# A block with attention and a gated MLP on one core: a one-tile first block, another order of loads and transposes, and more gate tiles inside the attention

## The chip, the core and the metric

The kernel runs on one core of a Trainium2 chip. The core has five engines, each with an instruction queue of its own that it works off in order: TensorE (PE) multiplies matrices out of SBUF into PSUM (eight banks of 128 partitions by 512 floats), VectorE (DVE) and ScalarE (ACT) read and write PSUM and SBUF, GpSimd (POOL) works on SBUF alone, SyncE (SP) issues DMAs. Engines wait for each other by semaphores. The metric is the device time of one execution in microseconds, the median of the runs; lower is better.

## The reference

One sequence of S = 2048 tokens, D = 448 features, all in bfloat16:

```
mod = silu(c) @ w_mod               # six vectors sa, ca, ga, sb, cb, gb of 448
h = layernorm(x) * (1 + ca) + sa
q, k, v = split(h @ wqkv)           # 16 heads of 28
p = softmax(q k^T / sqrt(28)), each query sees itself and the 255 keys before it
x = x + ga * ((p v) @ wo)
h = layernorm(x) * (1 + cb) + sb
z = gelu(h @ w_in)                  # 448 -> 1792
z1, z2 = halves of z;  z2 = layernorm(z2)
g = w_sp @ z2 + b_sp                # over the 2048 tokens
x = x + gb * ((z1 * g) @ w_out)     # 896 -> 448
```

## The kernel before

Tokens lie in 16 tiles of 128. With a window of 256, a query tile j needs the key tiles j-2, j-1 and j. The work goes through these parts, which overlap:

- **Projection by blocks of tiles** (lines 574 to 742): blocks of 2, 2, 2, 2, 4 and 4 tiles. `ln1` takes statistics of each tile on VectorE (line 543), the reciprocal root by a `pow` on POOL (551), and writes the normalised tile `xn`. The tile must then be turned, features on partitions: in the first four blocks by TensorE against an identity, with the eviction applying the modulation (`transp_pe`, 600; evictions at 622 and 626), in the last two by a DMA transpose from SP with a `modulate` on VectorE or POOL behind it (`transp_dma`, 637; 633). `project` (697) makes Q and K in eight chains of four matmuls per block, moving 128 columns per tile of the block, evicted at 718 and 721, and V in four matmuls of 448 columns per tile, evicted at 729 and 732. The weights `WQK` are copied from the loaded `wqk_raw` into padded form first (650 to 659).
- **Attention by query tile** (771 to 843). For each key tile one score block of 16 small matmuls fills two pairs of banks (`s_fn`, 781), one pair for eight heads; one exp on ScalarE evicts a pair (796), so a tile has up to three score blocks and six exps, 90 exps in all. POOL masks the tiles at the edges of the window (804). Eight matmuls multiply an exp's result by V (a PV unit, 809); VectorE divides by the sum (826, 829), a DMA transpose turns the result (833), four matmuls multiply it by `wo` (839), and VectorE adds x (842). Score blocks take their banks from the pairs (0,1), (2,3), (4,5); most projections take single banks from 6, 7, 4, 5.
- **The gated part** (869 to 943). After the second layernorm, z2 of a tile is a `Pair` (662) of chains that share a pass of half-height matmuls, seven passes of 448 columns; z1 of four tiles is seven chains of 512 columns. Their gelu is on ScalarE (899, 918). The tiles in `zraw` (here 0 and 1) are evicted without gelu into the z2 buffer by VectorE or ScalarE (888 to 892), so that the exp table stays loaded, and ScalarE applies gelu there later (895).
- **Mixing over tokens and the output** (970 to 1008). 28 chains of 16 matmuls of 512 columns (980), then the output matmuls (1000), the last addition (1005) and the stores.

The order of all this is not found at run time. Every piece of work is an operation with a number, and the list `ORDER` names them one by one: an engine executes its own operations in the order of the list, `.1` picks another engine where an operation allows one, and the numbers behind a slash pick PSUM banks or buffers. `schedule` (79) reads it, `emit` (102) derives the waits from the data and the buffers. Names such as `qk3_1` (block 3, chain 1), `S2_2` (tile 2, second score block) or `E0_1` (an exp) are those that the code gives to the operations. `warm` operations (1023 to 1027) are matmuls on zeros that fill TensorE's time while the loads come in. Loads (469 to 479) go out from SP, two from ScalarE.

Of the kernel before, what the change touches and what calls it, by code (L numbers as in the profile page):

```python
# [4 lines left out]
ACT = mybir.ActivationFunctionType  # L5
# [50 lines left out]
class Planner:  # L56
# [108 lines left out]
0 16 7 1 21 20 17 18 26 23 28 27 118 120 2 3 1673/0 1674 1675 1676 1677 1678 1679 1680 1681 1682 1683 1684 1685 29/2 1686 1687 1688 1689 1690 1691  # L165
1692 1693 1694 25 30 1695 32/1 33 34 31 8 9 14 6 10 5 4 12 15 13 11 50 119 51 121 54 52 122 53 19 22 55 123 24 56 58/0 124 57 125.2/4 126.2/1 35 1696
1697 1698 1699 1700 36 37 1701 60/0 38 1702 1703 39 59/3 127/0 131/2 40 41 49 46 45 48 47.1 128 61 62.1 63.1 65/1 1704 64 1705 1706 132 1707 1708 1709
66 67 134 129.1 130.1 42 43 44 323 319 321 325 324 326 320 322 327 93/3 88/7 98/0 89 90 103/2 104 99 100 101 91 94 83/1 105 68/6 69 106 70 84 102 92
107 133 85 71 78/7 86 79 95 96 80 81 87.1 72 97 73/0 74 82 75 76 113/6 114 115 116 252 185 77 487/0,1 488/3 491/6 328 329 330.1/1 117.1 333.1/4
332.1/3 489 492 331.1/2 1710 108/4 109 110 1711 140/1 111 141 142 1712 1713 143 145/0 146 147 1714 1715 1716 148 502/1,0 112 155/2 156 157 158 186 254  # L170
253 255 187 402 188 189 404 159.1 403 256 144 149 485/1 135/0 136 1717 137 138 1718 165/2 166 167 168 506/0 503/1 486 509/0,1 139 169 493/0 490 170/2
171 1719 1720 172 180/1 181 182 183 173 160/3 161 162 163 510/7 512/9 184 522/0,1 150/1 151 152 153 494 495/1 257 258 507 504 190 408 406 174.1 191
334 336 337 496/1 335 154.1 505/0 513 511 508 407 514 515/2 405 164 526/10 523/3 529/1,2 530/7 192.1/3 193.1/0 259.1/4 175/1 176 177 178 179.1 516/0
533/1 194/0 195 409 196 197 536/0,1 198/1 199 200.1 201.1 222/3 497/2 498 499 500 207/0 223 208 209 210 224 202/1 203 225 539/4 537/5 211 226 549/0,1
553/8 550/6 260.1/1 531 410 501 932 265/2 204 205 206.1 212/3 232/0 213 214 215 233 266 234 235 216.1 517/1 518 519 520 227/3 521 534 524 411 412 554
527 413.1/3 415.1/0 236 268 267 556/1,0 560/0 557/9 228 229 230 538/0 237/2 217/1 525 238 239 231.1 934 218 219 262/3 261 220 240 532 535 340 241.1
221 264.1 263.1 563/1,0 540 528 564/2 566/4 269/1 242/3 314/2 243 270 315 316 317 244 245 576/1,0 541 933 935 542/2 318.1 936 246.1 577/5 580/3 294/0
295 271 272 296 247/2 297 279/3 248 249 280 281 250 273.1 274/1 275 276 282 277 419 543/1 903 900 902 901 298.1 283.1 278.1 251 583/1,0 284/0 299/2
300 301 302 285 286 287 584/7 587/10 303.1 289/1 290 291 292 288.1 590/1,2 591/1 416.1/2 561 558 414.1/1 551 418 339.1 937 341.1 567/0 555 552 938
293.1 939/2 581 578 941/0 588 585 338.1 559 565 562 593/6 603/1,0 544/1 545 546 547 607/8 604/4 568 569/2 548 917/0 918 919 920 921 922 610/2,0 611/9  # L180
923 924 614/2 925 926 309/1 310 311 312 313.1 579/0 589 617/1,2 594 304/1 305 306 586 307 592 582 947 308.1 420 417 612 423.1 605 615 940 570/1 595
596/1 948 906 618/10 620/0 630/1,0 634/5 631/3 347/1 348 349 352/3 571/2 353 354 355 342/0 350 572 637/0,1 573 574 356.1 421 575 351 638/1 641/6 343
344 345 357/1 358 346.1 644/0,2 359 360 621/0 613 616 606 619 645/7 647/2 657/1,0 661/9 658/4 949 950 361.1 951 362/1 635 608 609 622 623/2 632 942
944.1 952 642 953 956.1/2 954.1/1 422.1 639 662 363 387/2 364 388 389 392/3 393 365 372/0 394 366 664/1,0 668/0 665/10 373 390 391.1 669 367/1 368 369
374 370 371.1 395 396.1 424 375 1410 904 1409 597/3 907 598/2 599 1408 624/2 909 943.1 659 957 955 960.1 666 671/0,1 376 674/8 600 601 636/0 377/1 378
379 648 602 672/5 684/1,2 380 685/2 633 640 646 643 688/7 381.1 691/1,0 625/1 626 627 628 649 650/2 629 397/0 398 399 400 401.1 692/1 695/6 698/2,1
382/1 383 384 385 699/3 908 910 905 651/0 911 912 673/0 701/5 660 675 711/0,2 715/4 712/8 386.1 962 964 663 670 667 963 676 677/1 430/1 431 432 433
718/1,2 652/0 653 654 655 434.1 965 966 656 977 978 450/1 451 719/9 722/10 686 693 945.1 689 696 961.1 713 723 716 958.1 720 725/1,0 678/3 914 913
1415 1414 452 714/0 728/0 435/3 436 437 438 729 460/2 453 461 726/8 454 738/1,0 742/0 727 721 739/8 717 724 425/1 426 427 428 462 463 429 745/1,0 967
439.1 968 971/1 969/0 740 730 731/2 749/9 746/10 694/0 690 679/1 680 681 682 464.1 683 979 980 981 982 743 747 750 702 752/2,0 755/4 697 455/1 456 457  # L190
458 687 753/5 765/1,0 700 459.1 703 704/0 445/1 446 447 448 769/1 766/7 772/2,0 773/3 776/6 946.1 732/1 733/0 734 735 736 970 972 1412 1411 705/0 1413
449.1 737 959 983 994 440/1 441 442 779/2,1 782/2 756/0 744 748 741 443 751 780/4 444.1 792/0,1 754 757 758/1 465/1 466 467 468 796/10 799/1,2 793/8
469.1 995 470/0 471 472 473 800/0 986/0 767 777 984/1 770 774 474.1 803/9 480/1 481 482 483 806/0,1 775/0 778 781 771 783 768 484.1 784 785/2 807/5
809/4 819/2,0 823/3 475/1 476 477 478 804 801 794 797 973.1 479.1 987 976 974 808/0 802 798 820/6 826/0,1 810 795 805 830/1 824 821 831 827/2 759/1
915 985 916 828 760/1 761 762 763 811 812/1 833/1,2 764 1007 1008 836/9 825/0 832 927/1 834/5 846/0,2 847/4 850/0 822 837 835 829 853/1,0 929 838
839/0 857/3 854/8 786/3 813/2 1419 1416 840/1 1417 706/3 707 814/2 708 815 816 709 990.1 991.1 988.1 817 860/0,1 975.1 848 858 851 989.1 855 931 930
928 710 818 992 993 996 863/1 861/10 852/0 787/1 788 789 790 849 873/2,1 859 864 856 862 791 997 998 865 866/2 874/2 877/9 875 880/0,2 841/1 842 843
844 884/7 878 876/0 881/4 1001/0 845 885 999/2 882 879 887/1,2 890/3 888/9 1298/3 1300 1307/4 1301/5 1308 1299 1068/2 1072/3 1309 1310 886 1069 883
1071 1154/1 1070 889 891 1303 1302 1073 1156 1311 1074 1160 1304 1157 1009 1010 1011 1022 1024 1025 1023 1012 1013 1014.1/1 1026 892 893/1 867/2 1002
1000 1076.1 1306 1075.1 1305 1158 1280/4 868/3 1159 1155 869 870 871 1161/1 1077/2 1052/2 1098/3 1284/5 1102 1281 1103 1100 1015 894/0 1016.1/0 1027  # L200
1028 872 1017 1162 1005.1 1003.1 1029/2 1004.1 1427 1436 1030 1163 1164 1079 1031.1/1 1078 1032 1080 1037 1081 1020.1 1056/3 1101 1084/1 1086 1057
1283 1099 1087 1088 1104 1090 1286 1058 1105/0 1282 1285 1055 1089 895/1 1085 1312/2 896 1053 897 1288 1287 1091/3 898 1054 1289/4 1315/5 1292/6 1165
1038 1106 1107 1108 1006.1 1082 1166 1019 1083 1059.1 1060.1 1061/2 899 1039 1290 1294 1317 1314 1321/1 1316 1293 1330/0 1334/7 1331 1318 1327/3 1295
1336 1313 1333 1291 1322 1335 1323 1325 1332 1320 1296 1297 1319 1112/0 1326 1324 1117 1115 1113 1018.1 1021.1 1339/6 1114 1371/2 1329 1328 1337 1040
1041 1092 1093 1042 1043 1109 1094 1095 1062 1063 1432 1437 1035.1 1046/0 1110 1044/1 1033.1 1111 1064 1167 1036 1065 1066 1067 1353/3 1372 1340 1373
1374 1126/2 1341 1354 1130 1342 1116 1338 1375 1118 1132 1359/2 1344/7 1356 1357 1131 1119/1 1343 1127 1196/0 1358 1198 1128 1355 1348/6 1129 1200
1201 1199 1349 1346 1345 1347 1202 1350 1197 1361 1133/0 1360 1420 1439 1426 1047 1045 1433 1425 1121 1049 1120 1122 1134 1048.1 1051.1 1034.1 1096
1050.1 1135 1136 1123 1097 1137 1124 1138 1224/2 1229 1225 1228 1140/3 1141 1143 1227 1226 1203/2 1205 1125 1230 1146 1142 1376/4 1380/5 1378 1144
1351 1231/3 1352 1379 1252/2 1257 1256 1204 1206 1207 1233 1208 1209 1139 1362/7 1145 1147/1 1253 1365/6 1255 1254 1368 1258 1382 1259/0 1366 1364
1367 1381 1394/3 1398/2 1168/2 1363 1377 1395 1399 1170 1370 1383 1384 1369 1396 1172 1169 1403/6 1173 1404 1397 1171 1182/0 1400 1402 1401 1423 1422  # L210
# [873 lines left out]
```

## Time and profile before

| what | value |
|---|---|
| median of 3 runs | 280.18 us (279.99 to 280.56) |
| span of the profiled execution, first to last instruction | 279.1 us |
| PE, ACT, DVE, POOL busy | 268.0, 135.4, 156.1, 94.2 us |
| first exp starts | 17.77 us |
| exps busy | 84.4 us, 90 of them |
| granted TensorE clock | 1.00 in every stage |

The page gives no total of its own for the profiled execution; its span is what the stages are cut from, and the time around the span is taken from the runs' median. Busy shares are averages over stages with different limits, so the table alone does not say what holds the kernel: the chain of waits and the stages do. A row of a timeline reads: start and length in us, engine, line, operation, output <- inputs by the program's names, shape, count. Many rows show line 435, the helper that records every matmul; they are told apart by the tiles' names.

### The profile page before, as it was taken

The numbers are of one execution on the slowest core, as the hardware profiler recorded it, in microseconds if no ns is written. First come the engines' busy times: TensorE is split into PE (matmuls) and PEld (weight loads), VectorE is DVE, ScalarE is ACT, GpSimd is POOL, SyncE is SP. The second block draws the span as 40 slices with busy tenths as digits, with TensorE's granted clock in tenths as the row PEclk, the third lists the DMA queues.
The fourth block names the chain that finished last, engine by engine and source line by source line (L and its number), as shares of the span: only waits on it lengthen the run. The fifth ranks groups of instructions, "written<-read, shape, count | busy, mean of one in ns | idle before, by whom it ended". The sixth has DMA issues, their size and how long they took to land.

```text
span 279.1 us, 6498 instructions
## 1 busy us (share of the span) xinstructions
PE 268.0 (96%) x2750; PEld 142.8 (51%) x2776; DVE 156.1 (56%) x373; ACT 135.4 (49%) x183; POOL 94.2 (34%) x156
## 2 busy tenths in 40 slices
PE   8899999999999988999999999999999999999995
PEld 4667677655565645444344444444444444444452
DVE  5688775576757688597385841332424230433543
ACT  4689999999999999866566600000000000000000
POOL 4166796755568677646322120000000000000000
PEclk9999999999999999999999999999999999999999
DMA  7954129796587683469999700000000000000223
GB/s 240 366 125 76 23 42 203 131 168 161 145 152 133 126 154 77 94 113 169 172 167 189 133 4 0 0 2 0 0 0 0 19 0 0 2 0 0 66 79 105
DMA packets 67503, 25.38 MB, mean 91 GB/s; under 512 B 56337, under 2 KB 67346, under 8 KB 67474
## 3 DMA queue, kind: packets, MB, share of 16 engines
q1 hardware_dynamic: 67200, 24.50, 42.5%
q8 instruction: 22, 0.36, 0.6%
q10 hardware_dynamic: 274, 0.46, 0.5%
q14 instruction: 7, 0.06, 0.1%
HBM read 9.48 MB, written 1.84 MB: 41 GB/s over the span
## 4 chain that ended last, share of the span: by engine, by line
PE 79%; ACT 16%; DMA 2%; issue 1%; DVE 1%; SPq 0%
PE ps L435 79%; ACT PT L796 13%; DMA wmod_sb<-in_w_mod_dram 2%; ACT hT L622 2%; ACT QKT L718 1%; SPq L466 0%; DVE fin L1005 0%; DVE x_sb L842 0%; DVE st_all L543 0%; ACT Vaug L729 0%
## 5 line engine op out<-in xcount | busy, mean ns | idle before, releaser
L796 ACT ACTIVATE PT<-ps 128x1024 bf16<-128x1024 f32 x90 | 84.4, 1078 | 2.6 <-PE ps L435 2.3
L986 DVE TENSOR_TENSOR tmpg<-ps,bsp_bc 128x512 bf16<-128x512 f32 x28 | 19.3, 691 | 59.2 <-PE ps L435 59.2
L435 PE MATMUL ps<-QKT,z 128*128 128x512 bf16 x219 | 50.7, 379 | 0.3
L804 POOL TENSOR_SCALAR_AFFINE_SELECT PT<-PT 128x512 f32<-128x512 f32 x60 | 37.2, 638 | 11.3 <-ACT PT L796 11.3
L435 PE MATMUL ps<-hT,WQK 128*128 128x256 bf16 (+1 forms) x182 | 34.6, 305 | 2.2 <-ACT hT L622 0.8
L435 PEld LDWEIGHTS ps<-QKT,z 128*128 128x128 bf16 x224 | 21.9, 98 | 26.4
L551 POOL TENSOR_TENSOR rs_all<-ve_all,neghalf 128x1 f32<-128x1 f32 (+2 forms) x31 | 20.0, 650 | 38.1 <-DVE ve_all L550 37.8
L435 PE MATMUL ps<-w_in_sb,hT 128*128 128x448 bf16 (+1 forms) x128 | 29.2, 353 | 0.1
L435 PE MATMUL ps<-hT,w_in_sb 128*128 128x512 bf16 (+1 forms) x106 | 27.5, 379 | 0.5 <-DVE st_all L543 0.3
L435 PE MATMUL ps<-w_spC,z 128*128 128x512 bf16 x110 | 26.7, 379 | 0.1
L435 PE MATMUL ps<-w_spD,z 128*128 128x512 bf16 x109 | 26.1, 379 | 0.2
L435 PEld LDWEIGHTS ps<-Vaug,PT 128*128 128x128 bf16 x720 | 22.7, 97 | 5.8 <-ACT PT L796 0.4
L435 PE MATMUL ps<-Vaug,PT 128*128 128x29 bf16 x720 | 25.0, 176 | 0.5 <-POOL PT L804 0.2
L543 DVE BATCH_NORM_STATS2 st_all<-z2raw 128x6 f32<-128x448 bf16 x32 | 18.6, 615 | 10.4 <-ACT z2raw L899 10.3
L435 PEld LDWEIGHTS ps<-hT,WQK 128*128 128x128 bf16 x192 | 16.9, 97 | 10.8 <-ACT hT L622 1.8
L435 PE MATMUL ps<-w_out_sb,z1T 128*128 128x448 bf16 x112 | 22.3, 352 | 0.0
L633 POOL TENSOR_SCALAR hT<-hT,modT 128x256 bf16<-128x256 bf16 (+1 forms) x31 | 18.5, 601 | 10.8 <-DMA hT<-xn 10.8
L564 POOL TENSOR_SCALAR xn<-x_sb,rs_all,nm_all 128x512 bf16<-128x512 bf16 x23 | 17.5, 769 | 8.0 <-DVE nm_all L555 4.3
L543 DVE BATCH_NORM_STATS2 st_all<-x_sb 128x6 f32<-128x448 bf16 x32 | 18.9, 615 | 1.7 <-DMA x_sb<-in_A_x_dram 1.5
L435 PE MATMUL ps<-QKT 28*128 28x128 bf16 x720 | 18.1, 217 | 1.7 <-ACT PT L796 1.3
L721 DVE CAST QKT<-ps 128x256 bf16<-128x256 f32 (+1 forms) x27 | 14.2, 531 | 8.3 <-PE ps L435 7.9
L918 ACT ACTIVATE z1T<-ps 128x512 bf16<-128x512 f32 x28 | 15.6, 600 | 5.8 <-PE ps L435 5.7
(70 smaller groups left out, 273.3 us busy)
## 6 DMA issues: line engine op xcount, KB each, us to landing
wmod_sb<-in_w_mod_dram SPq DMA_DIRECT2D x8, 224.0 KB, 4.0
w_in_sb<-in_B_w_in_dram SPq DMA_DIRECT2D x8, 224.0 KB, 3.8
out_dram<-fin SPq DMA_DIRECT2D x16, 112.0 KB, 1.7
x_sb<-in_A_x_dram SPq DMA_DIRECT2D x3, 448.0 KB, 8.3
wqk_raw<-in_A_wqkv_dram SPq DMA_DIRECT2D x2, 452.0 KB, 7.3
bsp_bc<-in_B_b_sp_dram SPq DMA_DIRECT2D x1, 512.0 KB, 5.8
x_sb<-in_A_x_dram SPq DMA_DIRECT2D x2, 224.0 KB, 3.3
wmod_sb<-in_w_mod_dram ACTq DMA_DIRECT2D x1, 448.0 KB, 4.5
```

The costliest lines, as they stand in the source:

```text
L435: return e.matmul(out_, lhsT=lhsT, rhs=rhs, start=st, stop=sp, **kw)
L543: st = [dve("%sst%d" % (name, i), prio, dve_ns(D), lambda e, i=i, s_=s_: e.bn_stats(st_all[:, slot, t, i, :], s_()), deps, tens) for i, s_ ...
L551: r = pool(name + "rs", prio, 420 + 148 * n, lambda e: e.tensor_tensor(rs_all[:, slot, t0:t1], ve_all[:, slot, t0:t1], neghalf[:, t0:t1], ...
L564: return e.tensor_scalar(dst, src, rs_all[:, slot, t:t + 1], nm_all[:, slot, t:t + 1], ALU.mult, ALU.add)
L622: return e.activation(hT[:, c_, cols], ps[:, ten.slot, q * 256:q * 256 + 256], ACT.Identity, bias=modT[:, c_:c_ + 1], scale=modT[:, 4 + c_ ...
L633: return e.tensor_scalar(hT[:, c_, cols], hT[:, c_, cols], modT[:, base_col + 4 + c_:base_col + 5 + c_], modT[:, base_col + c_:base_col + ...
L718: return e.activation(QKT[:, g, cols], ps[:, ten.slot, 0:w], ACT.Copy)
L721: return e.tensor_copy(QKT[:, g, cols], ps[:, ten.slot, 0:w])
L796: e_op = P.op("E%d_%d" % (j, ui), pr, [("act", 925, lambda e, ten=ten, pt=pt: e.activation(PT[:, pt.slot, :, :], ps[:, ten.slot:ten.slot + ...
L804: ready = pool("M%d_%d" % (j, ui), pr - 50, pool_ns(512), lambda e, pt=pt, pat=pat, cm=cm, cmp=cmp: e.affine_select(out=pt32(pt.slot), in_ ...
L918: g = P.op("z1g%d_%d" % (tb, ft), pr - 19, [("act", act_ns(512), lambda e: e.activation(z1T[:, ft, tb * 512:(tb + 1) * 512], ps[:, ten.slo ...
L986: a = dve("ga%d_%d" % (tb, ft), pr, dve_ns(512), lambda e, tb=tb, ten=ten, tg=tg: e.tensor_tensor(tmpg[:, tg.slot, :], ps[:, ten.slot, :], ...
```

## The change

What it does:

- The blocks are 1, 1, 2, 4, 4, 4 tiles. The first three (tiles 0 to 3) are turned by TensorE, the block of tiles 4 to 7 now by DMA transposes from SP, like the last two.
- In a first block of one tile, each of the four feature chunks has a PSUM bank and an eviction of its own; in the others one operation holds the two evictions of a bank.
- The score block of tile 0 is split into two halves by heads, each needing half of the Q and K chains and followed by its own exp; the PV matmuls of tile 0 take the heads in that order.
- Tile 0 and tile 1 of x are loaded separately. The order list issues the loads as x0, x0b, w_mod, x (tiles 2, 3), the two halves of `wqk`, x (4 to 7), part of `wv` and so on. The code's `order=` on them sets no semaphore.
- The two operations that move the modulation columns out of PSUM become one addition of a small constant tile, set by two memsets on POOL.
- `zraw` holds five tiles, 0 to 4. In the order list, tiles 0 to 3 stand on TensorE ahead of tile 14's score blocks; before, all z2 tiles stood behind tile 15's last score block. Nine z1 matmuls also move ahead of that block.
- 30 warm matmuls, the first 12 of 512 columns, instead of 44 of 256 and four groups of 16 small ones.
- The list `ORDER` is another one throughout; which engine does an eviction, a copy or a norm is chosen anew (for example two `WQK` copies on POOL). Orders between z2 or z1 and score blocks that only the writer of the list used are dropped.

TensorE's queue from the list after the change, around tile 2 (x4 is four matmuls of a chain): `S2_0 qk2_7x4 qk2_6x4 v3x4 PV1_2 PV1_1 qk3_1 S2_2 PV1_0 PV1_3 qk3_1 qk3_0x4 wo0x3 S2_4`.

```
 PARAMS = {
-    'blocks': (2, 2, 2, 2, 4, 4),
-    'by_pe': (1, 1, 1, 1, 0, 0),
+    'blocks': (1, 1, 2, 4, 4, 4),
+    'by_pe': (1, 1, 1, 0, 0, 0),
...
-    'zraw': (0, 1),
+    'zraw': (0, 1, 2, 3, 4),
...
-    x0 = load_x("x0", -99, 0, 2)
-    t_wmA = load_dup("wmodA", -98, wmod_sb, w_mod, 0, 2 * D, engs=("sp", "act"), rate=290.0)
+    x0 = load_x("x0", -99, 0, 1)
+    x0b = load_x("x0b", -99, 1, 1, [x0])
+    t_wmA = load_dup("wmodA", -98, wmod_sb, w_mod, 0, 2 * D, engs=("sp", "act"), rate=290.0, order=[x0b])
...
-        return [dve(name + "e0", prio + 0.01, 80, lambda e: e.tensor_copy(modT[0:w, col:col + 4], ps[0:w, ten.slot, 0:4]), ops, [ten]),
-                dve(name + "e1", prio + 0.01, 80, lambda e: e.tensor_scalar(modT[0:w, col + 4:col + 8], ps[0:w, ten.slot, 4:8], 1.0, None, ALU.add),
-                    ops, [ten])], ops
+        return [dve(name + "e", prio + 0.01, 80, lambda e: e.tensor_tensor(modT[0:w, col:col + 8], ps[0:w, ten.slot, 0:8], zero_one[0:w, :], ALU.add),
+                    ops + t_zo, [ten])], ops
...
-        for half in range(2):
+        per = 1 if b == 0 and n == 1 else 2
+        for u in range(4 // per):
             ten = Ten(B_ALL if b == 0 else B_D, guard=True)
...
+            def f_d(e, ev=ev):
+                for d, s_, k, a in ev():
+                    last = e.tensor_scalar(d, s_, k, a, ALU.mult, ALU.add)
+                return last
...
+                halves = [[Ten(banks((a, a + 1))) for a in a_] for a_ in ((0, 2), (4, 6))] if j == 0 else [tens]
+                for gs, tens in zip(((0, 1), (2, 3)) if j == 0 else ((0, 1, 2, 3),), halves):
+                    deps = [QK_op[(g, blk[j])] for g in gs] + [QK_op[(4 + g, blk[kb])] for g in gs]
...
-                    h = 4 * g + 2 * gp + s_
+                    h = 4 * (2 * gp + g % 2) + 2 * (g // 2) + s_ if j == 0 else 4 * g + 2 * gp + s_
...
-    for i in range(44):
-        if i in (10, 12, 13, 20):
-            warm_ops.append(pe("warmt%d" % i, 999, 300, warm_fn(2 if i == 12 else 1), [t_warm], [w_ten], order=warm_ops[-1:]))
...
+    for i in range(30):
+        n_ = 512 if i < 12 else 256
```

More of the change, by code (lines that the diff above doesn't have):

```diff
@@ L169 @@
[L169 to L176, printed above, removed]
@@ L607, in transp_pe, with fn @@
                 t = t0 + i
-                def fn(e, t=t, i=i, half=half, ten=ten):
+                def fn(e, t=t, i=i, u=u, ten=ten):
                     last = None
-                    for c_ in (2 * half, 2 * half + 1):
-                        q = c_ % 2
-                        last = mm(e, ps[:, ten.slot, q * 256 + i * 128:q * 256 + (i + 1) * 128],
+                    for q in range(per):
+                        c_ = per * u + q
+                        last = mm(e, ps[:, ten.slot, (q * n + i) * 128:(q * n + i + 1) * 128],
@@ new lines, in transp_pe, with ev, f_a @@
+                mms.append(pe("tr%d_%d_%d" % (b, u, i), pr + u * 0.01, 60 * per, fn, [xn_op[t], t_ident], [ten, xn_ten[t]]))
+            def ev(u=u, ten=ten):
+                for q in range(per):
+                    c_ = per * u + q
+                    yield (hT[:, c_, t0 * 128:(t0 + n) * 128], ps[:, ten.slot, q * n * 128:(q + 1) * n * 128],
+                           modT[:, 4 + c_:5 + c_], modT[:, c_:c_ + 1])
+            def f_a(e, ev=ev):
+                for d, s_, k, a in ev():
+                    last = e.activation(d, s_, ACT.Identity, bias=a, scale=k)
+                return last
@@ L631, in modulate @@
+            def f_d(e, ev=ev):
+                for d, s_, k, a in ev():
+                    last = e.tensor_scalar(d, s_, k, a, ALU.mult, ALU.add)
+                return last
+            op = P.op("hT%d_%d" % (b, u), pr + 0.1, [("act", per * (act_ns(128 * n) + 90), f_a), ("dve", per * (dve_ns(128 * n) + 50), f_d)],
+                      mms + t_modA, [ten], hold=1000 * per + 128 * n)
+            for q in range(per):
+                hT_op[b][per * u + q] = op
     def modulate(name, prio, c_, cols, n, base_col, deps):
@@ L788, in s_fn @@
                     return last
-                deps = [QK_op[(g, blk[j])] for g in range(4)] + [QK_op[(4 + g, blk[kb])] for g in range(4)]
-                s_op = pe("S%d_%d" % (j, ui), pr - 50, 270, s_fn, deps, tens, mode=32, order=all_S[-1:])
-                s_op.scores = 2
-                all_S.append(s_op)
-            S_op[(j, ui)] = s_op
-            ten = tens[gp]
-            pt = Ten(rot("pt", NPT))
-            e_op = P.op("E%d_%d" % (j, ui), pr, [("act", 925, lambda e, ten=ten, pt=pt: e.activation(
-                PT[:, pt.slot, :, :], ps[:, ten.slot:ten.slot + 2, :].rearrange("p b n -> p n b"), ACT.Exp, scale=SCALE))],
-                [s_op, t_exp0], [ten, pt], table="exp")
+                s_ops = []
@@ L799, in bass_adaLN_cond__sliding_block__mixer_gmlp__prompt_kernel @@
+            S_op[(j, ui)] = s_ops[-1]
+            e_op = P.op("E%d_%d" % (j, ui), pr, [("act", 925, lambda e, e_in=e_in, e_out=e_out: e.activation(
+                e_out(), e_in(), ACT.Exp, scale=SCALE))], [s_op, t_exp0], e_tens + [pt], table="exp")
             E_op[(j, ui)] = e_op
-            e_op.scores = -1
             ready = e_op
```

189 lines of the change are left out of this document (95 added, 94 removed), and 4 rows, old and new, of the table PARAMS.

## The prediction

> **What bounds the kernel now.** I read the page first, then the chain of waits in order of time, then the busy time by stage, then timelines of single stretches.
>
> ```profile
> PE   8899999999999988999999999999999999999995
> ACT  4689999999999999866566600000000000000000
> ...
> PE 79%; ACT 16%; DMA 2%; issue 1%; DVE 1%; SPq 0%
> ```
>
> TensorE looks full in every slice, ScalarE full in the first 40%. The chain says where each holds:
>
> ```profile
> 1.81 6.14 DMA wmod_sb<-in_w_mod_dram
> ...
> 11.17 3.28 ACT hT L622 x7
> ...
> 14.49 8.47 PE ps L435 x91
> ...
> 80.62 23.95 ACT PT L796 x26
> ...
> 110.56 5.83 PE ps L435 x57
> ```
>
> Loads until 8 us, the first block's evictions on ScalarE until 14.5, then TensorE, exps from 80 to 108, then TensorE to the end. The stages, cut at score blocks (a score block is a row of 16 matmuls 28x128; the first of tile 0 starts at 17.32, of tile 4 at 40.38, of tile 10 at 77.6, the last of tile 15 at 109.89):
>
> ```profile
> 17.30:40.40 23.10, 22.33 (x370) 15.78 (x373) 18.21 (x48) 22.32 (x33) 18.86 (x28) 1.00 0.23 44
> 40.40:77.60 37.20, 36.17 (x691) 22.70 (x696) 25.46 (x58) 36.00 (x41) 23.77 (x39) 1.00 0.82 162
> 77.60:109.90 32.30, 29.90 (x674) 19.14 (x678) 23.64 (x50) 31.67 (x36) 23.09 (x38) 1.00 0.70 126
> ```
>
> The columns after the length are PE, PEld, DVE, ACT, POOL. ScalarE is busy 31.67 of 32.30 us in the third stage, TensorE is not. Busy time counts a matmul's drain, so I price TensorE by pitch, (stretch minus mean of one) / (count - 1):
>
> ```profile
> 10.11 0.72 PE L435 MATMUL ps<-ident,xn 128*128 128x128 bf16 x10
> ...
> 39.34 1.11 PE L435 MATMUL ps<-wv_sb,hT 128*128 128x448 bf16 x5
> ...
> 43.44 1.49 PE L435 MATMUL ps<-hT,WQK 128*128 128x256 bf16 x12
> 44.85 0.40 PE L435 MATMUL ps<-QKT 28*128 28x128 bf16 x16
> 45.19 1.37 PE L435 MATMUL ps<-Vaug,PT 128*128 128x29 bf16 x48
> ...
> 168.57 6.21 PE L435 MATMUL ps<-QKT,z 128*128 128x512 bf16 x28
> ```
>
> With the groups' means (219, 353, 273, 176, 379 ns) that is 0.056 us for 128 columns, 0.11 for 256, 0.216 for 512, 0.189 for 448, 0.20 for a PV unit of 8. A score block costs 0.34 to the next work plus 0.1 ahead of it: 0.44.
>
> **TensorE work by stage, before.** Counted along its queue in the order list. Stage 1 (17.32 to 40.38): 66 QK matmuls of 256 columns 7.2, 20 V 3.8, 9 score blocks 4.0, 12 PV units 2.4, 16 transposes 0.9, gate 0.8, 8 wo 1.5, 11 warm matmuls 1.2: 21.7 of 23.1, so 1.4 of waiting. Stage 2: 36.6 of 37.2, waits 0.6. Stage 3: 28.8 of 32.3, waits 3.5; there the exps hold. Stage 4 (109.89 to the last matmul at 276.27): 163.5 of 166.4, waits and array switches 2.9. The tail, last eviction and store, is 279.12 - 276.27 = 2.85. The sum is the span. The runs' median, 280.18, stands 1.06 above this span; I carry that over.
>
> **The change up to the first scores.** By the time the QK weights are in, the same bytes stand ahead of them as before (x tiles 0 to 3 448 KB, w_mod 896, QK 904), so I keep their landing: before, the first copy of them starts at 10.62. Only w_mod has 224 KB less in front, about 0.6 us at the 366 GB/s of slice 2, and lands near 7.3 instead of 7.95. After the modulation columns (8.7) tile 0's four evictions of 128 columns (ScalarE three, VectorE one; 0.35 to 0.45 each, from 0.58 and 0.53 at 256) end by 10; before, seven of 256 columns ran from 11.15 to 14.43 on ScalarE. VectorE then copies three pieces of WQK, to 11.65; 16 QK matmuls of block 0 end at 12.6, 12 of block 1 at 13.3. The first half score block needs a QK eviction that VectorE does behind one 0.6 us stats operation: 13.5, and the first exp at 14.0 instead of 17.77. The one merged modulation add replaces two of 0.16 and 0.15; the two zero_one memsets (0.4 each at most) fall in POOL's 3.28 us of idle before its first pow. Two WQK copies move to POOL, where the trace has none: between VectorE's 0.29 and POOL's 0.77 for 128x512; even 2 x 0.77 from 10.5 ends at 12.1, before their first reader at 13.8. Tile 0's two exps read two bank pairs by a longer pattern, at between the 0.92 of any exp and, if the pattern breaks the stream, twice that; I take 0.92, and the other end is 1.8 us on ScalarE where it idles anyway. The warm-up stands where TensorE waits for loads anyway.
>
> **Stage 1 after.** Work: QK 36 of 128 columns 2.0, 32 of 256 3.5, 32 of 512 6.9; V 24 4.5; scores 8 x 0.44 + 2 x 0.34 = 4.2; PV 2.4; transposes 0.45; gate 0.8; wo 4 0.8: 25.5, 3.8 more than before, since block 3 (tiles 4 to 7) must be projected before tile 4, and less was done before the first scores. The waits that the order puts in: the second half block stands behind VectorE's chain of stats and evictions (4.4 us from 12.6: five stats-size steps, seven small evictions), so it runs at 17.1, not 16.4, and the next exp at 17.5; block 2's second half stands behind VectorE at 20.3; and the first matmul of block 3, queued on TensorE ahead of tile 2's second score block, needs a modulate of the DMA transposes. Their input is normalised at 19.5 to 21.7, SP issues four at 1.25 each (before: three in 4.45), the last lands near 25.9, VectorE gets to the second modulate at 28.6, TensorE is there at 27.8. Together 2.75 us of waits, worked out by hand; the ends are 0 and 5.5. Tile 4's scores: 13.5 + 25.5 + 2.75 = 41.75, 1.4 later than before. So the early start is not kept; ScalarE idles in between.
>
> **Stage 2 after.** 36.5 (QK 12.1 instead of 13.2, four more wo), waits 0.6: tile 10 at 78.85.
>
> **Stage 3 after.** Less 10 QK (2.2) and 3 PV (0.6), plus four gate tiles of 7 matmuls of 448 (28 x 0.189 = 5.3) and nine z1 matmuls (1.9): 33.3. Exps cannot fill more than before: 8 in 7.65 us, 0.92 apart, 34 of them 31.2 and two copies. So TensorE is now the longer by about 1 us, and before's 3.5 of waits has work in it. The remainder lies between 0 and 3.5; with the engines so close I take 1.5, nearer to zero as stage 1 and 2, where TensorE led, show 1.4 and 0.6. Tile 15's last scores: 78.85 + 33.3 + 1.5 = 113.65. The gate tiles' ten raw evictions are seven on VectorE (0.62), three on ScalarE (0.54); VectorE is busy 23.64 of 32.30, so there is room.
>
> **Stage 4 after.** 163.5 - 5.3 - 1.9 + 2 PV 0.4 = 156.6, waits 2.9 kept: 273.15. Tail 2.85: span 276.0, median 277.1. The fifth gate tile is evicted raw in this stage and saves nothing. The w_sp transposes queue on SP behind tile 15's output transpose, about 10 us later than before; at the 1.45 us each of 124.56 to 156.42 the last that the first columns need lands near 154, and TensorE asks at about 160: hidden.
>
> **A rule beside it.** The trace shows the array's cold and warm pace: ten weight loads of warm-up in 1.84 us from 1.36, 0.19 apart, and seven in 0.67 from 6.31, 0.10 apart. The Trainium skill (TensorE: Matmul & The Clock Gate, Part 1: The HAM clock gate) says that an idle window of about 3.4 us puts the array back to half its clock. After the change TensorE has about 2 us with nothing to do, 9.6 to 11.65, where before the longest pause, 6.98 to 7.99, left the pitch at 0.056. By that rule nothing happens unless the thin work around it counts as idle.
>
> **Rivals.**
> - Early waits vanish (0 for 2.75): 274.3. For it: ScalarE and VectorE have shorter evictions; against: the order above.
> - The late waits stay at 3.5 and the gate tiles only move work: 279.1. For it: the gate tiles take banks 4, 5 and 7, two of which are the third pair for scores.
> - The array falls to half pace after the pause: about 3.4 us of work then takes 1.7 longer: 278.8.
> - Early waits twice mine (5.5): 279.8, no change. VectorE's in-order queue is the cause then.
> - Slower: the first gate tile stands on TensorE ahead of tile 13's scores and needs all of w_in; the last pieces, with w_out (1,232 KB), are issued behind tile 8's output transpose, from about 86.2. At the 150 GB/s of these slices they land at 94.4, and TensorE gets there near 95. Each us later stops TensorE and, behind it, the exps. From a landing after 98.7 (100 GB/s) it is slower than before; at 101 it gives 282.5. For it: before, a 336 KB piece took 4.2 us alone; against: before's pieces landed within 4.2.
>
> **Chances.** Forecast 0.42, early waits gone 0.13, late waits stay 0.10, half pace 0.04: faster by over 0.2% (0.56 us, about what a measurement here can tell) 0.69. Early waits doubled 0.16: same. Late load 0.15: slower. The range, 274.0 to 281.0, leaves out most of the late load and a little of the first rival.
>
> **What would show it.** First scores near 13.5 and first exp near 14.0; tile 4's scores near 41.8; ScalarE with about 3 us of idle before it; TensorE's work, not exps, on the chain from 42 to 113; the last scores near 113.7; no wait of TensorE for w_in. Wrong, if tile 4's scores come before 39.5 or after 44, if TensorE stands at the gate tiles, or if the columns wait for w_sp.

## The result and the profile after

The changed kernel takes 285.24 us in the median of nine executions (282.08 to 287.36), the kernel before, on the same chip, 280.28 (279.99 to 282.12). The ratio is 1.0121, with a 95% interval of 1.0086 to 1.0156; it leaves out three executions at the lowest mean clock as disturbed, which are more of the effect told below. The forecast was 277.1 us and the range ended at 281.0: the kernel is slower, where 0.69 stood on faster. The profiled execution took 282.84 us, with a span of 281.1, so 2.4 us under the median.

The page of the changed kernel, the same rows as before: through the attention (the third to the sixteenth slice) TensorE had nines and two eights before and now has four eights and a seven among its nines, and ScalarE has fewer nines. In the chain, DMA has gone from 2% to 11%.

```profile
PE   7689899998998799999999999999999999999995
ACT  5589798999899969894876610000000000000000
PEclk9999999999999999999999999999999999999999
...
PE 77%; DMA 11%; DVE 6%; ACT 2%; POOL 2%; issue 1%; SPq 0%; DVEq 0%
```

The stages of the changed kernel, cut at the same score blocks (length, then PE, PEld, DVE, ACT, POOL busy, clock, DMA share, GB/s):

```profile
13.78:41.90 28.12, 26.25 (x382) 15.73 (x381) 21.76 (x58) 24.15 (x38) 17.74 (x25) 1.00 0.43 80
41.90:80.31 38.41, 37.02 (x689) 21.14 (x689) 29.29 (x67) 35.23 (x40) 22.22 (x35) 1.00 0.54 118
80.31:118.51 38.20, 34.44 (x684) 20.17 (x682) 28.36 (x61) 33.81 (x37) 24.71 (x41) 1.00 0.65 119
118.51:281.10 162.59, 159.57 (x832) 72.15 (x831) 78.29 (x183) 31.94 (x48) 16.72 (x29) 1.00 0.33 64
```

First scores at 13.78 (forecast 13.5), tile 4's at 41.90 (41.75), tile 10's at 80.31 (78.85), the last at 118.51 (113.65), and 162.59 from there to the end (162.35). Against before, 3.5 us are won ahead of the first scores and 6.6 after the last; 5.1, 1.2 and 5.9 are lost in the three stages between, 2.0 in all. What TensorE stood for, longest sum first, in the changed kernel (us in total, times, longest):

```profile
PE ps L435 <- DMA oT<-o_sb: 3.8, 4, 1.6
PE ps L435 <- DVE WQK L666: 2.5, 1, 2.5
...
PE ps L435 <- DVE hT L642: 1.1, 1, 1.1
```

The first row is new: before, TensorE stood for no output transpose `oT`. The largest sum then was this, and 0.52 us its longest stand in the attention:

```profile
PE ps L435 <- ACT PT L796: 2.3, 7, 0.5
```

Now three of the four stands for `oT`, 3.3 us, lie in the third stage. In its timeline they are the matmuls with `wo`, and the pause of 2.5 us is in front of the first block's QK matmuls:

```profile
11.92 1.93 PE L435 MATMUL ps<-hT,WQK 128*128 128x128 bf16 x28 [2.52 <-DVE WQK L666]
...
87.41 0.92 PE L435 MATMUL ps<-wo_sb,oT 112*128 112x448 bf16 x4 [1.12 <-DMA oT<-o_sb]
...
98.49 0.93 PE L435 MATMUL ps<-wo_sb,oT 112*128 112x448 bf16 x4 [1.64 <-DMA oT<-o_sb]
```

The chain of waits goes through the second of these (start, length, what). SP began to issue the transpose of tile 10's output at 92.13, was done with that at 93.80, and the transpose landed at 98.44, 4.6 us later. The text below counts a landing from the end of the issue.

```profile
92.13 6.31 DMA oT<-o_sb
98.44 0.05 issue
98.49 12.54 PE ps L435 x220
```

### The profile page after: what moved, and what is told of

It is laid out like the page before. It is cut to its first block, busy times and chain, and to the rows that moved or that the text cites. A ratio compares the mean times of both kernels' runs of the same rounds, so it can differ in the third digit from the quotient of the medians.

```text
span 281.1 us, 6350 instructions
## 1 busy us (share of the span) xinstructions
PE 266.8 (95%) x2682; PEld 135.2 (48%) x2682; DVE 167.5 (60%) x396; ACT 133.0 (47%) x176; POOL 86.6 (31%) x144
## 4 chain that ended last, share of the span: by engine, by line
PE 77%; DMA 11%; DVE 6%; ACT 2%; POOL 2%; issue 1%; SPq 0%; DVEq 0%
PE ps L435 77%; DMA oT<-o_sb 7%; ACT PT L825 2%; DMA hT<-xn 2%; DMA wmod_sb<-in_w_mod_dram 2%; DVE st_all L544 1%; DVE hT L642 1%; POOL xn L565 1%; DVE QKT L730 1%; POOL PT L831 1%; DVE o_sb L856 1%; DVE WQK L666 1%; DVE hT L633 1%; SPq L466 0%; DVE rec_all L853 0%
## 5 line engine op out<-in xcount | busy, mean ns | idle before, releaser
L825 ACT ACTIVATE PT<-ps 128x1024 bf16<-128x1024 f32 x90 | 85.8, 1038 | 10.6 <-PE ps L435 10.1
L435 PE MATMUL ps<-QKT,z 128*128 128x512 bf16 x224 | 49.0, 379 | 0.0
L435 PE MATMUL ps<-hT,WQK 128*128 128x512 bf16 (+2 forms) x192 | 34.5, 308 | 3.7 <-DVE WQK L666 2.5
L435 PE MATMUL ps<-w_in_sb,hT 128*128 128x448 bf16 (+1 forms) x128 | 28.2, 353 | 0.0
L435 PE MATMUL ps<-w_spC,z 128*128 128x512 bf16 x112 | 25.5, 379 | 0.0
L435 PE MATMUL ps<-w_spD,z 128*128 128x512 bf16 x112 | 25.2, 379 | 0.0
L1032 DVE TENSOR_TENSOR fin<-ps,x_sb 128x448 bf16<-128x448 f32 x16 | 9.9, 623 | 18.8 <-PE ps L435 18.8
L435 PEld LDWEIGHTS ps<-hT,WQK 128*128 128x128 bf16 x192 | 14.4, 97 | 12.8 <-DVE WQK L666 2.7
L435 PE MATMUL ps<-wo_sb,oT 112*128 112x448 bf16 x64 | 15.3, 353 | 3.8 <-DMA oT<-o_sb 3.8
L730 DVE CAST QKT<-ps 128x512 bf16<-128x512 f32 (+2 forms) x28 | 14.8, 540 | 5.1 <-PE ps L435 5.0
```

The costliest lines, as they stand in the source:

```text
L435: return e.matmul(out_, lhsT=lhsT, rhs=rhs, start=st, stop=sp, **kw)
L730: return e.tensor_copy(QKT[:, g, cols], ps[:, ten.slot, 0:w])
L825: e_op = P.op("E%d_%d" % (j, ui), pr, [("act", 925, lambda e, e_in=e_in, e_out=e_out: e.activation(e_out(), e_in(), ACT.Exp, scale=SCALE)) ...
L1032: f = dve("fin%d" % t, pr, dve_ns(D), lambda e, t=t, ten=ten, ft_=ft_: e.tensor_tensor(fin[:, ft_.slot, :], ps[:, ten.slot, 0:D], x_sb[:, ...
```

## The experiments

Each kernel but the second starts from the changed one; "filled" means with the edit of e1. In the names of the order list, `oT10` is the output transpose of tile 10 and `wo10` the four matmuls behind it, `z2m0` the gate matmuls of z2 of tile 0, `hx8` an input transpose, and `win`, `wout`, `wmod` and `wsp` are loads of the weights (those of `w_sp` are transposes). Line 435 is line 436 in some of these kernels.

Each run lists the mean granted clock of every execution. It falls mostly in steps of 0.006; in the traces, a step is one stretch of 3.41 us at a clock of 0.50 (0.006 of 280 us is 1.7, half of 3.4). The last column counts a step as a stretch. An execution with a mean of 0.997 or more keeps the clock. Executions by their clock, medians in us:

```
kernel                        n   at 0.997-1   at 0.990-0.996   below     stretches
                                  n  median    n  median        n median  per execution
before (four sets)          100  69  280.31   24  281.90        7 283.48    0.39
changed (two sets)           21   5  282.27    9  284.19        7 285.92    1.14
e10 thinner                  12   0            4  283.61        8 285.70    1.92
e2 before, thin              10   0            5  280.29        5 281.47    1.50
e1 filled                    10   7  280.52    3  282.71        0           0.30
e8 half filled               12   8  280.69    3  283.97        1 284.31    0.42
e3 filled, loads             10   8  280.91    2  282.78        0           0.20
e6 filled, wmod              12   8  281.03    4  282.65        0           0.33
e9 filled, wmod, wo          12   8  282.16    4  283.90        0           0.33
e4 filled, wo later           4   2  283.07    1  285.83        1 287.43    0.75
e7 filled, gates back         6   0            0                6 291.75    3.33
e11 filled, loads, wmod, wo  12  12  281.63    0                0           0.00
e12 filled, loads, wmod      12  12  279.76    0                0           0.00
```

The experiments ran on four chips, where the kernel before took 280.48 to 281.08 in the median, so medians of different chips compare to some 0.6 us, and the ratios to the kernel before are the better guide there.

**e1, the pause filled.** 21 more warm matmuls of 256 columns stand where TensorE idles before the first projection.

```
-    mm(e, ps[:, w_ten.slot, 0:n_], warm[:, 0:128], warm[:, 0:n_], True, True)
+    [mm(... the same ...) for _ in range(22 if i == 29 else 1)][-1]
```

> The changed kernel with 21 more warm matmuls of 256 columns (2.3 us) in TensorE's pause from 9.2 to 11.9 us; nothing else moves, since the QK matmuls wait for the WQK copies until 11.9. Theory A (part of the loss is the clock: the pause lets the array fall to half pace for one or two stretches of 3.4 us, as the mean granted clocks of the nine executions, 1.00, 0.994 and 0.988, suggest): the clock is 1.00 in every execution, the spread shrinks from 5.3 us to under 1, and the median is near 282.3, still 2 above the kernel before, with tile 15's last scores near 118.5. Rival B (the clock differs for another reason, and the spread with it): clocks below 0.995 in about two thirds of the executions as before, median 284 to 285.5.

Measured 281.31 us (279.28 to 283.01), ratio 1.0013 (0.9974 to 1.0052): 3.9 us less than the changed kernel's 285.24, by adding work. Seven of ten executions keep the clock. At full clock it is 280.52 against the changed kernel's 282.27, so not all of the gain is the clock.

**e2, the kernel before with a thin warm-up.** `warm14` to `warm32` of the kernel before are cut to one column.

```
-    mm(e, ps[:, w_ten.slot, 0:256], warm[:, 0:128], warm[:, 0:256], True, True)
+    mm(... 0:n_ ...)        with n_ = 1 if 14 <= i < 33 else 256
```

> The kernel before with 19 of its warm matmuls (the ones between 6.3 and 11.3 us) cut from 256 columns to 1. Nothing that is needed is late, because TensorE waits for loads there. Theory A: thin work counts as idle, the clock falls in some executions, and those take 1.5 to 3.5 us longer; median 281 to 283. Rival B: clock 1.00 throughout and the median within 0.5 us of 280.2.

Measured 281.05 us (279.75 to 282.34), ratio 1.0015 (0.9982 to 1.0047). No execution keeps the clock; the trace of this kernel has the stretch here:

```profile
5.97:9.39 3.42, 2.35 (x82) 1.94 (x75) 2.97 (x15) 1.65 (x4) 1.90 (x3) 1.00 1.05 390
9.39:12.80 3.41, 3.29 (x27) 2.31 (x28) 2.78 (x9) 3.25 (x7) 0.00 (x0) 0.50 1.10 350
```

So a thin warm-up loses the clock in the kernel before too. But there the stretch lies beside the loads and evictions that hold the start anyway (first scores at 16.86, before 17.32), and the median does not move by what can be told here (1.50 stretches per execution for 0.39). When a stretch comes counts as much as whether it comes.

**e3, filled, and loads moved out of the third stage's queue.** On SP:

```
-  ... win2_1 wout2 wout4 win3_1 win1_0 wsp0_4 oT10
+  ... oT10 wsp0_4      (the other five now behind wmod4, wmod5, wmod5, win2_0, wout0)
```

> e1 with five late loads (three pieces of w_in, two of w_out, 1.2 MB) and one w_sp transpose taken from directly ahead of tile 10's output transpose on SP: the loads go 11 to 43 us earlier, the transpose behind it. Theory C (wo stands on TensorE because its DMA transpose lands late behind these loads): tile 10's output transpose lands within 2.5 to 4.5 us of its issue instead of 6.3, TensorE's 1.6 us at wo of tile 10 goes, time 1.5 to 2 us under e1. Rival D (transposes take 4 us now and then whatever stands ahead, so that wo is simply asked too early): under 0.7 us of gain, and the waits of TensorE for output transposes stay above 2.5 us in total.

Measured 281.13 us (279.27 to 283.37), ratio 0.9996 (0.9952 to 1.0040), no gain that can be told from e1. oT10 now landed 1.2 us after its issue and TensorE did not stand for it, and the third stage is 36.0 us; but in e1's profile, with the loads unmoved, it is 35.9, and oT10, 2.8 us after its issue, was in time there. In the timeline of this kernel something else lay over it:

```profile
50.66 0.24 PE L436 MATMUL ps<-sc_sb,wmod_sb 128*128 128x1 bf16 x4 [1.83 <-DMA wmod_sb<-in_w_mod_dram]
...
51.17 0.85 PE L436 MATMUL ps<-sc_sb,wmod_sb 128*128 128x1 bf16 x28
51.88 1.61 PE L436 MATMUL ps<-wv_sb,hT 128*128 128x448 bf16 x4
```

A stand of 1.83 us for the later modulation weights, 32 matmuls of one column around a score block, and then four `wv` matmuls take 1.61 in place of 0.92: the clock was 0.50 from 51.95 to 55.37.

**e4, filled, four `wo` later.** In TensorE's queue (each `wo` is four matmuls):

```
-  S7_2 wo4 PV6_0 ...     S11_0 wo9 ...     S12_4 wo10 ...     PV14_5 wo13 S15_2
+  PV6_5 wo4 S7_4         v13_3 wo9         S13_0 wo10         S15_2 wo13
```

> e1 with the four wo groups at which TensorE stood (tiles 4, 9, 10, 13) put 1.3 to 3 us later in its queue, each behind the next work that is ready; loads as in the changed kernel. Theories C and D both: TensorE's wait for output transposes falls from 3.8 us to under 1, the last scores of tile 15 come 3 to 4.5 us earlier (114 to 115.5), and the time is 3 to 4.5 us under e1, near 278. Rival E (ScalarE or the mask takes over as soon as TensorE stops waiting): last scores no earlier than 117, gain under 1.5 us.

Measured 284.64 us in only four executions (282.69 to 287.43), ratio 1.0109 (1.0022 to 1.0195): none of the gain that was expected, and 3.3 above e1 in the median, though the intervals overlap. In its profile, an execution with two stretches at half clock, the stands went from `wo` to score blocks and PV units (1.26 us at 88.1, 0.99 at 100.5).

**e5, the changed kernel again**, on the chip of e6 to e8.

> The changed kernel, unaltered, beside the fillings on one chip. Theory A (the thin warm-up costs the clock): median 283 to 286.5 us; most executions show a mean clock of 0.994 or 0.988, each 0.006 of it a stretch of 3.4 us at half clock, and each such stretch adds about 2 us; executions at 1.0 take 282 to 283. The output transposes that `wo` stands for (3.8 us in the profiled execution) should come to 1 to 4 us again. Rival (the 285.24 was a chance of that chip): median within 1 us of the filled kernel's 281.3.

Measured 284.03 us (280.80 to 285.92), ratio 1.0072 (1.0035 to 1.0109). The result repeats, and so does its size by the clock (table). This profile, with a span of 279.1, has a third stage of 36.1 us in place of 38.2: oT10 landed at 96.0 in place of 98.4. The exps show where that counts. In the changed kernel's first profile:

```profile
80.91 7.51 ACT L825 ACTIVATE PT<-ps 128x1024 bf16<-128x1024 f32 x8
88.72 7.58 ACT L825 ACTIVATE PT<-ps 128x1024 bf16<-128x1024 f32 x8 [0.30 <-PE ps L435]
96.90 1.94 ACT L825 ACTIVATE PT<-ps 128x1024 bf16<-128x1024 f32 x2 [0.59 <-PE ps L435]
100.96 1.94 ACT L825 ACTIVATE PT<-ps 128x1024 bf16<-128x1024 f32 x2 [2.13 <-PE ps L435]
```

and in this one:

```profile
80.96 15.00 ACT L825 ACTIVATE PT<-ps 128x1024 bf16<-128x1024 f32 x16
96.55 1.94 ACT L825 ACTIVATE PT<-ps 128x1024 bf16<-128x1024 f32 x2 [0.59 <-PE ps L435]
99.00 1.94 ACT L825 ACTIVATE PT<-ps 128x1024 bf16<-128x1024 f32 x2 [0.51 <-PE ps L435]
```

Until 96 the exps run end to end, whatever TensorE stands for: its 1.12 us at 87.41 cost ScalarE 0.30. From 96, where the gate tiles stand, ScalarE waits for TensorE, and the 1.64 us at 98.49 become 2.13 of idle where the second profile has 0.51. That lasts while the gate tiles stand there: from 108.5 to 116 the exps of the first profile run end to end again.

**e6, filled, modulation loads earlier.**

```
 SP: ... hx5 hx7 oT0
+    wmod3 wmod3 wmod4 wmod4
     hx8 hx9 oT1 hx11 hx10 oT2
-    wmod3 wmod3 wmod4 wmod4
```

> The filled kernel, with the four loads of the later modulation columns issued behind oT0 (SP idle from 27.1 to 31.3 us) and no more behind oT2 (44.0 us). Theory B (modB0 stands 0.8 to 1.8 us for these loads, ahead of S5_0, and now and then the clock falls there): the stand at modB0 gone, S10_0 0.8 us earlier than the filled kernel's 79.85, 280.3 us in all, clock 1.0 in nearly every execution. Rival F (another wait, of a score block or a `wo`, takes its place, the transposes hx8 and hx9 come 2 us later): within 0.3 us of 281.3.

Measured 281.34 us (279.44 to 283.56), ratio 1.0006 (0.9972 to 1.0040). The stand is gone and tile 10's scores start at 79.23, 0.63 earlier than in e1, as expected; but oT10 landed 3.9 us after its issue and TensorE stood 1.29 for it at 96.4. The total stays.

**e7, filled, the gate tiles back behind the attention.** The z2 matmuls of tiles 0 to 3, and their evictions, stand behind tile 15's last score block again.

```
-  S12_4 wo10 z2m0 PV12_3 ... S13_0 z2m2 ... S13_4 z2m1 z2m3 S14_0
+  S12_4 wo10 PV12_3 ... S13_0 ... S13_4 S14_0 ... S15_4 ... z2m0 z2m1 z2m2 z2m3 wo14
```

> The filled kernel, with z2 of tiles 0 to 3 put behind tile 15's last score block again, in front of wo14; their evictions go with them. Theory N (TensorE is the bound in the third stage, so the tiles only change place): S12_0 to S15_4 shrinks by 5 to 6 us from 24.9, from S15_4 to the end the time grows by as much, median 281 to 282. Rival G (they fill TensorE's waits for the output transposes and keep the clock up): S12_0 to S15_4 shrinks by 4 us only, stands at `wo` and at score blocks grow, 282.5 to 284 and clocks of 0.994 more often. Rival H (they delay the chain PV, division, transpose, `wo`): 279 to 280.5.

Measured 291.75 us (290.82 to 293.33), ratio 1.0374 (1.0327 to 1.0421), beyond all three expectations. Two windows, the second at half clock, and the waits of this kernel:

```profile
93.11:103.88 10.77, 7.92 (x194) 5.07 (x194) 9.19 (x18) 8.40 (x10) 6.74 (x11) 1.00 0.90 178
103.88:114.12 10.24, 7.61 (x131) 4.26 (x130) 4.17 (x10) 8.37 (x9) 7.96 (x14) 0.50 0.36 55
```

```profile
PE ps L436 <- ACT PT L826: 4.5, 5, 2.0
PE ps L436 <- DVE z L917: 1.8, 3, 0.7
PE ps L436 <- DMA oT<-o_sb: 1.4, 1, 1.4
```

Without these tiles TensorE stands for exps, and three stretches in a row run at half clock, so S12_0 to S15_4 takes 26.3 us where e1 with them takes 24.9. From the last scores to the end it is 9.2 us longer, four tiles of work and stands for evictions. This part of the change, in this order, is worth some 10 us. Part of that is the clock: 3.33 stretches per execution in place of e1's 0.30, at the 1.7 to 1.9 us that one costs the changed kernel some 5 to 6 us (an estimate). The theory that the tiles only change place falls, since they also keep TensorE from standing for exps; what they are worth at an even clock no run shows.

**e8, half the filling.** 10 more warm matmuls instead of 21 (`range(11 if i == 29 else 1)` in e1's edit); 1.38 us of the pause stay.

> The changed kernel with 10 more warm matmuls in the pause before the first block's projection in place of 21, so that some 1.2 us of the pause stays. Theory A1 (what counts is whether the pause is long): as the full filling, 281 to 281.6, clock 1.0 in two thirds of the executions. Rival A2 (the clock's loss goes with the idle time left): half-way, 283, with clocks of 0.994 in half of the executions or more.

Measured 281.67 us (279.49 to 284.31), ratio 1.0003 (0.9967 to 1.0038), as the full filling: with 1.38 us of the pause left, eight of twelve executions keep the clock, with all 2.5 us three of twelve on the same chip (e5). The profile has a stretch elsewhere, after a stand of 1.71 us at wo10 (97.9) among PV units:

```profile
98.86:102.27 3.41, 3.41 (x52) 1.98 (x50) 2.15 (x3) 1.14 (x2) 0.00 (x0) 0.50 0.72 154
```

**e9, as e6, three `wo` later.** Beside e6's edit:

```
-  S11_0 wo9 S11_2 ...   S12_4 wo10 z2m0x3 PV12_3 PV12_0 PV12_2 S13_0 ...   wo13 S15_2
+  S11_0 S11_2 wo9 ...   S12_4 z2m0x3 PV12_3 PV12_0 PV12_2 wo10 S13_0 ...   S15_2 wo13
```

> The filling and the earlier modulation loads, and in TensorE's queue wo10 behind three z2 matmuls and three PV units of tile 12 in place of right behind S12_4, wo9 behind S11_2 and wo13 behind S15_2 (some 1.3, 0.6 and 0.6 us later). Theory W (the stands at `wo` for an output transpose are lost time and, when long, pull the clock down): no stand over 0.5 us at a `wo`, S12_0 to S13_0 7 us or less (8.2 to 9.1 where oT10 landed late), 279.8 to 280.6 us, 0.8 to 1.5 less than the 281.34 with the loads alone. Rival X (the exps and the chain to the next bank set the pace, the stand only changes its name): stands at score blocks or PV units instead, 281 to 282.

Measured 282.89 us (280.73 to 285.33), ratio 1.0053 (1.0023 to 1.0083), 1.5 more than e6, on another chip (1.3 by the ratios). In the timeline of this kernel a score block stands at the place where wo9 did, for an exp, and PV units behind it:

```profile
84.83 0.40 PE L436 MATMUL ps<-QKT 28*128 28x128 bf16 x16
86.50 0.40 PE L436 MATMUL ps<-QKT 28*128 28x128 bf16 x16 [1.27 <-ACT PT L826]
```

```profile
PE ps L436 <- ACT PT L826: 2.0, 3, 1.3
PE ps L436 <- DVE o_sb L857: 2.0, 2, 1.3
```

The theory that a later place for `wo` saves the stand falls, as in e4.

**e10, thinner.** `warm17` to `warm29` of the changed kernel are cut to one column.

```
-    mm(e, ps[:, w_ten.slot, 0:n_], ... warm[:, 0:n_] ...)
+    the same with n_ = 1 if i >= 17 else n_
```

> The changed kernel with its last 13 warm matmuls of 256 columns cut to one column, so that TensorE has next to nothing from 6 us to the first projection at 12. Theory A (the thin stretch before the first projection makes the granted clock drop in the first 15 us): no execution at 1.0, most at 0.988 or below, the stretch of half clock shown between 8 and 16 us, the first score block 0.5 to 1.5 us later than 13.8, median 285 to 287. Rival A3 (the drops of the changed kernel arise in the attention, whatever stands before it): the same distribution as the changed kernel's, 284 to 285.

Measured 284.92 us (281.25 to 286.40), ratio 1.0089 (1.0049 to 1.0128). No execution keeps the clock. The stretch lies where it was expected, and the first 28 QK matmuls take 2.75 us in place of 1.93:

```profile
11.97 2.75 PE L436 MATMUL ps<-hT,WQK 128*128 128x128 bf16 x28 [3.47 <-DVE WQK L667]
```

```profile
12.47:15.88 3.41, 3.41 (x40) 3.02 (x38) 2.65 (x8) 2.20 (x7) 0.00 (x0) 0.50 1.11 335
```

The first score block comes at 14.66, 0.9 later than in the changed kernel. The median is 0.9 above e5's on another chip, 0.4 against the kernel before beside each, less than expected.

**e11, filled, with the moves of e3 and e6, and wo9 and wo10 later** (the edits of e1, e3 and e6, and two of e9's three).

> The filling, the earlier modulation loads, the earlier w_in and w_out loads of the third run, and wo9 and wo10 later. Theory W with a crowd on SP as a second cause of late transposes: 279 to 280, below the kernel before's 280.4. Rival X: 281 to 281.5.

Measured 281.63 us (280.66 to 282.74), ratio 1.0010 (0.9981 to 1.0039). Every execution keeps the clock, yet there is no gain: with wo9 late, a score block stands 1.27 us for an exp at 86.9 again, and the third stage is 37.6 us.

**e12, the same with every `wo` where the change has it** (the edits of e1, e3 and e6 alone).

> The filling, the earlier modulation loads and the earlier w_in and w_out loads with wsp0_4 behind oT10, and every `wo` where the change has it. So far oT10 landed 1.2 to 1.3 us after its issue in the three kernels with no weight load in flight at that time, and 2.0 to 4.6 us in the eight with some. Theory C (loads in flight hold up the output transpose, and with it the third stage): oT10 lands within 1.5 us, no stand over 0.3 us at wo10 or modB0, S10_0 to S15_4 35.9 us or less, clock 1.0 throughout, 279.5 to 280.5. Rival X (what goes at the `wo` comes back at score blocks): 281 to 281.7 as with the `wo` moved. Where the median lies under the kernel before's 280.4 by 0.5 or more, this is a version that beats both.

Measured 279.76 us (279.23 to 280.95), ratio 0.9967 (0.9941 to 0.9993) to a kernel before at 281.08 there. It beats the changed kernel, measured on other chips, by 4.3 to 5.5 us and, by a little, the kernel before. oT10 landed 1.2 us after its issue (91.50 to 92.72), 2.2 us before TensorE asked for it. The stands for `oT` are down from 3.8 us in all to 0.2, and the third stage is 35.34 us (37.6 in e11, which differs in the two `wo` alone):

```profile
79.11:114.45 35.34, 34.30 (x683) 20.06 (x681) 28.43 (x61) 33.48 (x37) 24.22 (x41) 1.00 0.68 95
```

The profile of e1 is 1.2 us longer: 0.9 of it in the second stage, where TensorE stood for the modulation loads, and 0.5 in the third.

## Why the prediction was wrong

Its own sum came to a span of 276.0; the profiled execution has 281.1, and the median lies at another 285.24. The difference of 8.1 us, step by step. The prediction priced TensorE's work; the rest is what remains of a stage beyond that work at the same prices.

- **The change up to the first scores: right** (13.78 for 13.5). ScalarE's evictions have left the chain.
- **Stage 1: right** (28.12 for 28.25, a rest of 2.6 for 2.75), also in its reason: the win of the start is lost again at the projection of tiles 4 to 7. It stood 1.08 us for a modulate at 28.82 (the 1.1 for `hT` above).
- **Stage 2: 1.3 short.** The rest is 1.9 for 0.6. TensorE stood 0.8 us for divided outputs and 0.5 for an output transpose; what else it holds is open.
- **Stage 3: 3.4 short, the step that failed.** "The remainder lies between 0 and 3.5; with the engines so close I take 1.5." The rest was 4.9 (38.20 less the 33.3 of work; the terms given add up to 33.2), and before it was 3.5: I had it shrink by 2.0, and it grew by 1.4. TensorE's time without a matmul says the same, 2.40 before (32.30 less 29.90, with a few matmul records missing from that trace) and 3.76 after. Half of the reasoning held: the gate tiles did fill the stands for exps, 1.6 us in this stage before and none after. What failed is that the 1.5 had no term for the output transposes, which came in their place with 3.3 us.

  Two things make the price. First, I gave the stage one bound. It has several in turn: exps until 96, TensorE until about 108, where the gate tiles stand, then exps again until 116. A stand of TensorE is nearly free beside the exps (0.30 of 1.12) and costs in full where the gate tiles stand (1.62 of 1.64).

  Second, the price there hangs on oT10. In the nine profiles of the changed queue with weight loads in flight when SP issued it (w_in, w_out and a w_sp transpose directly ahead), it landed 2.0 to 4.9 us after its issue and always after that w_sp transpose; in the four without such loads (before, e2, e3, e11) 1.2 to 1.3, and in e12, sent to test this, 1.2 again. The experiments moved the loads and the w_sp transpose together, so which of the two holds oT10 up is not shown. My slower rival had these loads late for the gate tiles; they landed by 94.9, in time, and what came late was the transpose behind them. So its "slower" came true by another cause. With loads and transpose moved the rest of the stage is 2.0 (e12), near the 1.5. e4 and e9 show that the `wo` cannot simply move back, e12 that the loads can.
- **Stage 4: right** (162.59 for 162.35). The w_sp transposes stayed hidden.
- **From span to run: 0.7 short.** I carried 1.06 over, the runs' median less the span of another execution. The executions listed with their span lie some 1.7 above it, so the profiled one of before would have taken some 280.8.
- **The clock: 2.4, put at a chance of 0.04.** The rival "half pace" asked for one early stretch in one case, and its price of 1.7 was right, though the stretch itself is 3.4 us long, not the work in it; the changed kernel has 1.14 stretches per execution, and an execution is 1.7 to 1.9 us longer for each (table). The median execution has one, the profiled one none; the other 0.5 of the 2.4 is spread among executions. Filling the pause alone brings the stretches to 0.3 (e1), fewer than the kernel before has (0.39); with both groups of loads moved as well, no execution of 24 has one (e11, e12). That the profile before shows no fall of the clock told nothing of the changed kernel: its warm-up was fuller, and its longest stand in the attention was 0.52 us.

The Trainium skill (TensorE: Matmul & The Clock Gate, Part 1: The HAM clock gate) gives a window of 3413 ns, free-running: the stretches of 3.41 us here agree. That such a window starts where it will in an execution would fit the difference between executions of one kernel, which no run here tests. Its rule of an idle window of some 3.4 us, taken as time without any matmul, does not agree: the longest stand in the five us before a stretch was 1.83 us in e3, 1.71 in e8 and 1.27 before the first one of e7, and in e2 0.84; only e10's pause, 3.47, is as long. So the condition at the end of "A rule beside it", that the thin work counts as idle too, fits what was seen.

What the change was good for is shown as well. Without the pause and with the loads out of the way (e12) it is at 279.76, and its gate tiles are worth some 10 us, part of it clock, against the same order without them (e7).

Open: where the changed kernel's own stretches lie, since both its profiles are of executions that kept the clock; that they follow the pause is shown by e1 and e8, and a place right behind it by the thinner e10 alone. At full clock the changed kernel is still 1.75 us above e1 (282.27 and 280.52, five and seven executions); 0.8 of it is there at tile 4's scores in the profiles, the rest is not explained. Nor is it shown that loads in flight alone make oT10 late: in the changed kernel and in e12 other output transposes take about 3 us with nothing in flight ahead of them. And e12 differs from e3 in the medians by 1.4 us, but the intervals of their ratios overlap.

## What to carry to other kernels

Where a stage changes its bound halfway, cut it there before adding up: here a stand of TensorE was nearly free while the exps ran end to end and cost in full once they didn't. Work that fills one wait can uncover another, so list what else the engine waits for there. Count the bulk loads and transposes that a queue holds ahead of a small transfer on the path, and try to move them before moving the work that waits. Warm-up work is part of the tuned kernel: before shortening it, list the pauses and thin stretches that it covered, and look at the granted clock of many executions, since one profile may show none of it. Compare an execution's time with its own span.

## What the hardware showed beyond that

- Half-clock stretches come in multiples of 3.41 us, in the middle of a kernel too: at 52 us after a stand of 1.83 (e3) or 1.27 (e7), at 99 after one of 1.71 (e8), and three in a row (10.24 us) from 103.9 in e7, after stands of 1.44 and 1.35 and with one of 2.05 among them. Stands as long are also followed by none: 1.64 at 98.49 in the changed kernel's profile, 1.29 at 96.4 in e6's.
- A stretch is worth 1.7 to 1.9 us on average in the changed kernel; one at 9.4 to 12.8, beside the loads, cost nothing that e2's median shows.
- Adding work in a pause made the kernel faster: 10 matmuls of 0.11 us by 2.4 us (e8 against e5, one chip), 21 by 3.9 (e1 against the changed kernel's 285.24).
- Other output transposes of the changed kernel land 1.2 or about 3 us after their issue with nothing in flight ahead of them (oT13: issued to 112.22, landed 115.08); before, those that took 2 us or more all had a load or a transpose in flight ahead, but so had some that took 1.2. Why is not known.
